# FNet mixing with windowed attention: the two lo-part differences of one weight tile are issued on DVE instead of GpSimd

## The chip, the core and the metric

The kernel runs on one core of a Trainium2 chip. Its time is the device time of one execution in microseconds (us). Before the change three runs gave 845.13, 845.97 and 846.19 us, a median of 845.97 us. The engines are called as the profile calls them: PE multiplies matrices, DVE (VectorE) and ACT (ScalarE) do elementwise work, POOL is GpSimd, and SP issues nearly all DMAs.

## The reference

```python
x = A_x                                              # 1 x 2048 x 512
g = sigmoid((x * gate_w).sum(-1, keepdims=True))
a = dft_seq_re @ (x @ dft_hid_re.T) - dft_seq_im @ (x @ dft_hid_im.T)
q, k, v = split(x @ wqkv)                            # 32 heads of 16
s = q @ k.T / 4, kept where 0 <= i - j < 256
b = softmax(s) @ v, heads joined, @ wo
return g * a + (1 - g) * b                           # 1 x 2048 x 512
```

## The kernel before, in words

Products of fp32 accuracy are made from fp32r pieces. Each operand X is split into `hi`, its value rounded to fp32r by a cast, and `lo = X - hi`, a difference. A product is then three matmuls (`TERMS`, L250): hi by hi, hi by lo and lo by hi. A weight tile (`raw`, 128x1024 fp32, two buffers) becomes a pair `hi`, `lo` (three buffers each) in four instructions: for each half of 512 columns one cast and one difference.

PE works through two streams at once. The dense stream (`dense`, L598) makes, in this order, the projections q and k of the first head group (`qk_proj(0, ss)`), the projection v of all rows (`v_proj`, sixteen calls of twelve matmuls of 512 columns each, into one PSUM tile `dv`), q and k of the second group (`qk_proj(1, ss, w)`, two chains of twelve matmuls, tiles `dqk`), the hidden transforms (`ab_proj`) and the sequence transforms. The attention stream makes for each query block n four score products (`s_pair`, L369), later their transposed form (`t_pair`) and the product with v (`pv`). The main loop interleaves them: `fill` takes dense matmuls between the attention's. Up to the block LAG = 19 the rhythm is one score matmul, then three dense ones. PE's order is written out by hand (`manual_schedule`, L993); DVE, ACT, POOL and SP are ordered by the framework's scheduler, and `behind(...)` (L68) ties an instruction to a place behind a named one of the same or another engine.

The PSUM tiles `d` of the dense stream have two buffers: a projection can begin when the one two before it has been evicted. A chain of q and k is evicted by ACT (`hi`, L88) and DVE (`lo`, L90 for k, L92 for q), a `dv` by ACT (L317). For each block DVE also makes the four masked scores (L371, from PSUM) and the padded weights of the next block's score matmuls (`make_pad`, L352, two instructions that read the SBUF tile `ring` and write the tile `pad`).

Small work is hung into the dense stream by a list `jobs`: `job` (L120) takes one entry off it at the third and ninth matmul of every twelve. `split_soon` (L111) puts the four instructions of one weight tile on the list: cast and difference of the first half, cast and difference of the second. On POOL's side it uses GpSimd up to block LAG (`masks` is still empty there) and DVE from then on. Each is issued through `late` (L588), which places it behind the last marked instruction of ACT and DVE, where its engine is one of these. For the second group's weights, at ss = 3, L623 sets an empty entry behind each of the four, so that they come twelve matmuls apart: in the `v_proj` of the row blocks 12, 13, 14 and 15. The second group's `qk_proj`, the first reader of the pair, follows at once.

The `raw` tile of these weights shares its two buffers with the tiles of `wi` (the imaginary hidden transform), which come in two loads, L631 and L641. The first is in place early. The second, called the second `wi` load here, takes the buffer of the second group's weights and so waits until their split has read it. Both `wi` tiles are split on POOL too. Their pieces are first read by `ab_proj(1, 0)`, whose matmuls begin at 108.6 us.

Of the kernel before, what the change touches and what calls it, by code (L numbers as in the profile page):

```python
# [32 lines left out]
def fnet_window_mix(ctx: ExitStack, tc: tile.TileContext, xT, x, wqk, wv, wr, wi, cr, ci, wo, gw, out):  # L33
    nc = tc.nc
# [23 lines left out]
    def f(ap):  # L58
        return ap.bitcast(F32)
# [7 lines left out]
    @contextmanager  # L67
    def behind(*engines):  # L68
        with ExitStack() as es:
            for e in engines:  # L70
                if e in last:
                    es.enter_context(tc.issue_after(last[e]))
            yield


    masks = []
# [19 lines left out]
    def load_raw(src):  # L96
        raw = st.tile([P, 1024], F32, name="raw", bufs=2)
        ld(raw, src)
        return raw
# [8 lines left out]
    jobs = []  # L108
    ended = []

    def split_soon(raw):  # L111
        hi = st.tile([P, 1024], F32R, name="hi")
        lo = st.tile([P, 1024], F32R, name="lo")
        for c in HALVES:
            jobs.append(lambda c=c: late(nc.scalar.copy if FIN else (nc.vector if masks else nc.gpsimd).tensor_copy,
                                         hi[:, c], raw[:, c]))
            jobs.append(lambda c=c: late((nc.vector if masks else nc.gpsimd).tensor_sub, lo[:, c], raw[:, c], f(hi[:, c])))
        return hi, lo

    def job(n):  # L120
# [26 lines left out]
    with tc.manual_schedule(engines={mybir.EngineType.Activation, mybir.EngineType.DVE, mybir.EngineType.SP}):  # L147
# [11 lines left out]
        for dk in range(DK):  # L159
            c = slice(dk * 256, dk * 256 + 256)  # L160
# [115 lines left out]
    def qk_proj(g, ss, w):  # L276
        for i in range(2):
            ps = ps_d.tile([P, 512], F32, name="dqk", tag="d")
            n = 0
            for dk in range(DK):  # L280
                c = dk * 256 + i * 128
                for a, b in TERMS:
                    nc.tensor.matmul(ps, w[a][:, c:c + 128], XT[dk, ss][:, b],  # L283
                                     start=n == 0, stop=n == 11)
                    n += 1
                    job(n)
                    if n < 12:
                        yield
            qk_evict(g, ss, i, ps)
            yield  # L290
# [22 lines left out]
    def v_proj(sb, w):  # L313
        ps = ps_d.tile([P, 512], F32, name="dv", tag="d")
        yield from row_proj(sb, w, ps)
        t = ev.tile([P, 512], F32, name="ev")
        mark("act", nc.scalar.copy(t, ps))  # L317
        ld(v_scr[sb // 2][sb % 2].rearrange("r a g x -> r (a g x)"), t)
        yield
# [182 lines left out]
    class Pieces:  # L502
# [8 lines left out]
        def split(self):  # L511
            if self.raw:
                k, raw = self.raw.pop(0)
                self.w[k] = split_soon(raw)
# [73 lines left out]
    def late(fn, *args):  # L588
        with behind("act", "dve"):
            return fn(*args)  # L590
# [7 lines left out]
    def dense():  # L598
# [10 lines left out]
        def x_job(ss, dk):  # L609
            late(split_x, ss, (dk,), ss == 1 or (None if ss == 3 else False))  # L610
            if dk % 2 and ss == 2:
                load_x(3, dk // 2)

        for ss in range(4):
            if ss < 3:
                for dk in range(DK):
                    jobs.append(lambda ss=ss, dk=dk: x_job(ss + 1, dk))
                    jobs.append(lambda: None)
            if ss:
                yield from qk_proj(0, ss, wq0)  # L620
            if ss == 3:
                w = split_soon(raw)
                jobs[:] = [j for split in jobs for j in (split, lambda: None)]  # L623
            for c in range(4):
                yield from v_proj(ss * 4 + c, wvs)
                have.add(("v", ss * 4 + c))
                if c == 1:
                    have.add(("qk", 0, ss))
                if ss == 2 and c == 2:
                    raw = load_raw(wqk[1])  # L630
                    wraw = [load_raw(wi[0])]  # L631
# [3 lines left out]
        for g in range(1, NG):  # L635
            for ss in range(4):
                yield from qk_proj(g, ss, w)
                have.add(("qk", g, ss))
                if g == 1:
                    if ss == 0:  # L640
                        wraw.append(load_raw(wi[1]))  # L641
                        ws = [split_soon(wraw[0])]
                    elif ss == 1:
                        ws.append(split_soon(wraw[1]))
                        raw = load_raw(wqk[2])
                elif g == 2:
                    if ss == 0:
                        raw = load_raw(wqk[3])
                        gate_soon(7)
                    elif ss == 1:  # L650
                        nextw = split_soon(raw)
                        wraw = [load_raw(wr[0])]
                    elif ss == 2:
                        wraw.append(load_raw(wr[1]))
                elif ss == 0:
                    ws = [split_soon(wraw[0])]
                elif ss == 1:
                    ws.append(split_soon(wraw[1]))
                    gate_load(4)
                elif ss == 2:  # L660
                    gate_load(5)
                else:
                    gate_soon(8)
# [9 lines left out]
            if g < 3:  # L673
                w = nextw
# [287 lines left out]


    stream = dense()
    quota = 0.0

# [150 lines left out]
```

## Time and profile before

| | |
|---|---|
| median of three runs | 845.97 us |
| the profiled execution's own time | 845.52 us |
| its span, first to last instruction | 843.6 us |
| granted clock of PE over the span | 1.000 |
| busy: DVE | 644.9 us (76%) |
| busy: ACT | 610.2 us (72%) |
| busy: POOL | 299.2 us (35%) |

Times in the rows count from the span's start. In a row of the timeline stand start, duration, engine, line and operation, the tile written and those read, the shape, and how many instructions were merged; in brackets the idle time of the engine ahead of it and what ended it. A matmul's duration contains its pipeline, so successive matmuls overlap, and the distance from start to start is what tells the rate.

### The profile page before, as it was taken

What the parts mean: (1) busy time and instruction counts of PE and PEld (TensorE: products, weight loads), DVE (VectorE), ACT (ScalarE), POOL (GpSimd) and SP (SyncE); (2) the same over time, 40 slices, a digit from 0 to 9 for tenths busy, and PEclk for the clock granted to TensorE, in tenths of its full rate; (3) what the DMA queues carried; (4) which work ended last, traced back from release to release, by engine and by line L of the source; (5) the groups of instructions that cost most, each with busy time, mean ns of one, the idle gap of its engine ahead of it and who ended that gap; (6) DMA issues with size and microseconds to landing.
All of it is one profiled execution on the core that took longest, in us unless ns stands there. A gap on an engine that the chain in (4) does not pass through costs nothing.

```text
span 843.6 us, 17198 instructions
## 1 busy us (share of the span) xinstructions
PE 838.4 (99%) x5322; PEld 697.5 (83%) x5322; DVE 644.9 (76%) x2082; ACT 610.2 (72%) x1832; POOL 299.2 (35%) x606
## 2 busy tenths in 40 slices
PE   9999999999999999999999999999999999999998
PEld 8887888888888888888888887878888878878997
DVE  5588978677879787787877876878987867666874
ACT  6487888878888897787977976867777865553430
POOL 8102332233232333242333243343232357756410
PEclk9999999999999999999999999999999999999999
DMA  8776678485765273544444557879874356456632
GB/s 310 238 225 179 219 247 278 165 246 215 221 221 184 58 225 108 178 124 121 140 150 136 166 149 229 288 223 300 284 216 140 99 179 203 140 184 205 217 132 94
DMA packets 94491, 161.03 MB, mean 191 GB/s; under 512 B 26816, under 2 KB 35520, under 8 KB 94400
## 3 DMA queue, kind: packets, MB, share of 16 engines
q1 hardware_dynamic: 93968, 159.28, 59.9%
q8 instruction: 42, 0.69, 0.3%
q10 hardware_dynamic: 432, 0.66, 0.2%
q14 instruction: 49, 0.40, 0.2%
HBM read 108.27 MB, written 51.64 MB: 190 GB/s over the span
## 4 chain that ended last, share of the span: by engine, by line
PE 98%; DVE 1%; DMA 0%; issue 0%; ACT 0%; DVEq 0%; ACTq 0%
PE dc L531 42%; PE dab L306 11%; PE dqk L283 10%; PE t L451 9%; PE s L369 8%; PE o L477 8%; PE dv L306 5%; PE t L926 5%; PE s L271 1%; DMA pt<-xT 0%; DVE pad L352 0%; PE s L389 0%; PE t L561 0%; ACT sm L374 0%; DVE sm L371 0%
## 5 line engine op out<-in xcount | busy, mean ns | idle before, releaser
L531 PE MATMUL dc<-big,hi 128*128 128x512 f32 x1020 | 344.6, 393 | 0.0
L371 DVE CUSTOM_DVE_ANT_0 sm<-s,mask 128x320 f32<-128x320 f32 (+4 forms) x512 | 235.2, 464 | 111.3 <-PE s L369 66.9
L374 ACT ACTIVATE sm<-sm,ml 128x320 f32<-128x320 f32 (+4 forms) x512 | 277.3, 543 | 58.3 <-DVE ml L371 53.7
L452 ACT ACTIVATE pt<-t 128x320 f32<-128x320 f32 (+4 forms) x392 | 159.5, 411 | 83.5 <-PE t L451 78.2
L531 PE MATMUL dc<-big,lo 128*128 128x512 f32 x510 | 200.2, 393 | 0.0
L531 PEld LDWEIGHTS dc<-big,hi 128*128 128x128 f32 x1020 | 179.3, 188 | 21.4
L456 POOL TENSOR_SCALAR_AFFINE_SELECT pt<-pt 128x128 f32<-128x128 f32 x196 | 77.0, 393 | 275.4 <-ACT pt L452 274.1
L451 PE MATMUL t<-ring,pad 128*128 128x320 f32 (+4 forms) x512 | 156.6, 306 | 0.0
L369 PE MATMUL s<-ring,pad 128*128 128x320 f32 (+4 forms) x512 | 155.0, 303 | 0.1
L352 DVE TENSOR_SCALAR pad<-ring,half 96x256 fp32r<-96x256 f32 x384 | 121.7, 363 | 5.2 <-PE t L451 4.9
L451 PEld LDWEIGHTS t<-ring,pad 128*128 128x128 f32 x512 | 96.1, 188 | 30.5 <-issue 9.1
L369 PEld LDWEIGHTS s<-ring,pad 128*128 128x128 f32 x512 | 96.2, 188 | 20.9 <-DVE ml L371 1.1
L531 PEld LDWEIGHTS dc<-big,lo 128*128 128x128 f32 x510 | 95.9, 188 | 11.9
L374 ACT ACTIVATION_READ_ACCUMULATOR sm<-sm,ml 128x1 f32 x512 | 97.4, 190 | 0.0
L590 DVE TENSOR_TENSOR lo<-raw,hi 128x512 fp32r<-128x512 f32 x137 | 95.1, 701 | 2.8 <-ACT hi L590 2.7
L306 PE MATMUL dab<-hi,big 128*128 128x512 f32 x256 | 88.9, 394 | 0.0
L283 PE MATMUL dqk<-big,hi 128*128 128x512 f32 x240 | 85.1, 393 | 0.0
L434 POOL TENSOR_SCALAR vpad<-vr,half 128x256 f32<-128x256 f32 x64 | 62.3, 986 | 62.3 <-PE o L477 29.6
L350 ACT ACTIVATE pad<-ring,half 96x256 fp32r<-96x256 f32 x128 | 66.7, 521 | 0.0
L456 POOL TENSOR_SCALAR_AFFINE_SELECT home<-home 128x128 f32<-128x128 f32 x60 | 34.5, 575 | 89.5 <-ACT home L452 87.0
L590 DVE CAST hi<-raw 128x512 fp32r<-128x512 f32 x126 | 53.7, 432 | 11.6 <-PE dc L531 10.6
L460 POOL TENSOR_SCALAR_AFFINE_SELECT pt<-pt 128x128 f32<-128x128 f32 x172 | 62.5, 363 | 0.0
(121 smaller groups left out, 1035.4 us busy)
## 6 DMA issues: line engine op xcount, KB each, us to landing
qk_scr<-home SPq DMA_DIRECT2D x32, 512.0 KB
ring<-qk_scr SPq DMA_DIRECT2D x32, 512.0 KB
raw<-cr SPq DMA_DIRECT2D x32, 512.0 KB
raw<-ci SPq DMA_DIRECT2D x32, 512.0 KB
r_scr<-ev SPq DMA_DIRECT2D x42, 256.0 KB
ab_scr<-home SPq DMA_DIRECT2D x20, 512.0 KB
big<-ab_scr SPq DMA_DIRECT2D x20, 512.0 KB
ring<-qk_scr SPq DMA_DIRECT2D x32, 256.0 KB
```

Source lines behind the costliest of these rows:

```text
L283: nc.tensor.matmul(ps, w[a][:, c:c + 128], XT[dk, ss][:, b], start=n == 0, stop=n == 11)
L306: nc.tensor.matmul(ps, XT[dk, ss][:, a, c * 128:(c + 1) * 128], wh[b], start=n == 0, stop=n == 11)
L352: mark(f"pad{i}", nc.vector.tensor_scalar(dst, src, half[:96, h:h + 1], None, op0=OP.mult))
L369: nc.tensor.matmul(ps[:, :w], PAD[0, n][:, p], ring[1][:, p, k0:k0 + w], start=True, stop=True)
L371: mark("dve", nc.vector.tensor_tensor_reduce(out=sm[:, :w], in0=ps[:, :w], in1=mask[:, WIN - w:], scale=1.0, scalar=3e38, op0=OP.add, op1= ...
L374: mark("act", nc.scalar.activation(sm[:, :w], sm[:, :w], AF.Exp, bias=nm[:, c], scale=-1.0, accum_out=l[:, c]))
L451: nc.tensor.matmul(ps[:, :w], PAD[1, n][:, p], ring[0][:, p, q0:q0 + w], start=True, stop=True)
L452: nc.scalar.activation(pt[:, p, :w], ps[:, :w], AF.Exp, scale=-1.0)
L456: nc.gpsimd.affine_select(a, a, pattern=[[0, 2], [2, 64]], compare_op=OP.is_ge, fill=0.0, base=1, channel_multiplier=-1)
L477: nc.tensor.matmul(OT[g, sb][32 * p:32 * p + 32, q - sb * 512:e - sb * 512], v2[:, p], pt[:, p, q - q0:e - q0], start=first, stop=kb == 8 ...
L531: nc.tensor.matmul(ps, w[a][:, i % 8 * 128:i % 8 * 128 + 128], ab[SC[i]][:, b], start=i == ends[0] and a + b == 0, stop=i == ends[1] and a ...
L590: return fn(*args)
```

## The change

`split_soon` gets a second argument. Where it is set, the two differences go to DVE whatever `masks` holds; the casts stay where they were. It is set in one of its calls, that for the second group's weights.

```diff
-    def split_soon(raw):
+    def split_soon(raw, on_dve=False):
         hi = st.tile([P, 1024], F32R, name="hi")
         lo = st.tile([P, 1024], F32R, name="lo")
         for c in HALVES:
             jobs.append(lambda c=c: late(nc.scalar.copy if FIN else (nc.vector if masks else nc.gpsimd).tensor_copy,
                                          hi[:, c], raw[:, c]))
-            jobs.append(lambda c=c: late((nc.vector if masks else nc.gpsimd).tensor_sub, lo[:, c], raw[:, c], f(hi[:, c])))
+            jobs.append(lambda c=c: late((nc.vector if on_dve or masks else nc.gpsimd).tensor_sub, lo[:, c], raw[:, c], f(hi[:, c])))
         return hi, lo
...
             if ss == 3:
-                w = split_soon(raw)
+                w = split_soon(raw, True)
                 jobs[:] = [j for split in jobs for j in (split, lambda: None)]
```

The orders of PE and ACT are the same in both kernels. On POOL, around the split of the second group's weights (`lo<-raw,hi` and `hi<-raw` are the instructions of all weight tiles; the first two casts are the second group's, the next ones those of `wi`), the difference between the two orders is:

```order
 L202 MEMSET ring_264 32x4x512
 L82 CAST big<-raw 128x512 x4
-L590 CAST hi<-raw 128x512 x2
-L590 TENSOR_TENSOR lo<-raw,hi 128x512 x2
-L590 CAST hi<-raw 128x512 x2
+L590 CAST hi<-raw 128x512 x4
 L590 TENSOR_TENSOR lo<-raw,hi 128x512
 L590 CAST hi<-raw 128x512
```

The two differences behind the first two casts are gone; the four casts stand in a row, and the three differences of `wi` keep their places.

On DVE the first of the two differences comes into the row block 13 of v. Before, from the last of the small transposed rows (L400; `ISA` is the masked score of L371 and the reading of its minimum) over the next pads (L352):

```order
L400 TENSOR_TENSOR mhl<-s,mhl 32x128
L371 ISA sm,ml<-s,mask 128x320
L371 ISA ml 128x1
L352 TENSOR_SCALAR pad_0_260<-ring_264,half 96x4x64 x2
L371 ISA sm,ml<-s,mask 128x320
L371 ISA ml 128x1
```

The same place now:

```order
L400 TENSOR_TENSOR mhl<-s,mhl 32x128
L371 ISA sm,ml<-s,mask 128x320
L371 ISA ml 128x1
L352 TENSOR_SCALAR pad_0_260<-ring_264,half 96x4x64 x2
L590 TENSOR_TENSOR lo<-raw,hi 128x512
L371 ISA sm,ml<-s,mask 128x320
```

The difference stands right behind a pair of pads. The second one stands in the same way behind the pair of pads two blocks later. On SP one load moves (`v_scr_119` and `v_scr_120` are stores of v, `raw<-wi` is the second `wi` load):

```order
 L56 DMA v_scr_119<-ev 128x512
 L56 DMA ring_264<-m_scr_141 4x4x512
+L56 DMA v_scr_120<-ev 128x512
 L56 DMA raw<-wi 128x1024
-L56 DMA v_scr_120<-ev 128x512 x2
+L56 DMA v_scr_120<-ev 128x512
 L56 DMA qk_scr_1_0_85<-home 128x2x512
 L56 DMA vr<-v_scr_113 128x4x64
```

The second `wi` load now stands behind the store of v's row block 14 instead of ahead of it, and waits for DVE instead of POOL.

## The prediction

> **What bounds the kernel now.** First the page's list of busy times, then the waits of PE alone.
>
> ```profile
> PE 838.4 (99%) x5322; PEld 697.5 (83%) x5322; DVE 644.9 (76%) x2082; ACT 610.2 (72%) x1832; POOL 299.2 (35%) x606
> ...
> PE dv L306 <- DVE home L90: 0.8, 1, 0.8
> ```
>
> PE is busy for 99% of the span, so an edit on DVE and POOL counts only where PE stands still for them. There is one such place in the list of PE's waits: a matmul of v waits once for DVE's eviction of a k chain (L90). The timeline of PE there, of which I took the score matmuls (one per round) and the matmul that waited:
>
> ```profile
> 68.01 0.31 PE L369 MATMUL s<-ring,pad 128*128 128x320 f32 x1
> 68.85 0.31 PE L369 MATMUL s<-ring,pad 128*128 128x320 f32 x1
> ...
> 69.23 0.40 PE L306 MATMUL dv<-hi,big 128*128 128x512 f32 x1
> 70.47 0.50 PE L306 MATMUL dv<-hi,big 128*128 128x512 f32 x1 [0.84 <-DVE home L90]
> 70.87 0.42 PE L369 MATMUL s<-ring,pad 128*128 128x320 f32 x1
> ...
> 72.05 0.42 PE L369 MATMUL s<-ring,pad 128*128 128x320 f32 x1
> ...
> 73.00 0.31 PE L369 MATMUL s<-ring,pad 128*128 128x320 f32 x1
> ...
> 73.84 0.31 PE L369 MATMUL s<-ring,pad 128*128 128x320 f32 x1
> ```
>
> A round of one score matmul and three of v takes 0.84 us (68.01 to 68.85, 73.00 to 73.84). From 68.85 to 73.00 there are three rounds, 2.53 us at that rate, and they took 4.15. So the stop cost **1.62 us**, not the 0.84 that the wait list shows: the two rounds behind it are slow too. Why was L90 late? DVE and POOL at the same moment, and DVE's pads one and three blocks away from it:
>
> ```profile
> 63.65 0.61 DVE L352 TENSOR_SCALAR pad<-ring,half 96x256 fp32r<-96x256 f32 x2
> ...
> 67.03 2.78 DVE L352 TENSOR_SCALAR pad<-ring,half 96x256 fp32r<-96x256 f32 x2
> 69.73 0.68 DVE L90 TENSOR_TENSOR home<-dqk,home 128x512 fp32r<-128x512 f32 x1
> ...
> 75.56 0.61 DVE L352 TENSOR_SCALAR pad<-ring,half 96x256 fp32r<-96x256 f32 x2
> 65.92 1.18 POOL L590 CAST hi<-raw 128x512 fp32r<-128x512 f32 x2 [28.20 <-PE dqk L283]
> 67.06 2.60 POOL L590 TENSOR_TENSOR lo<-raw,hi 128x512 fp32r<-128x512 f32 x2
> ```
>
> A pair of pads takes 0.61 us, this one 2.78, and it ends at 69.81, just behind POOL's two differences (67.06 to 69.66). They are the two that the change takes off POOL. The pads lost 2.17 us to them, L90 stood behind the pads, and PE's next `dv` needed the PSUM buffer that L90 frees: L90 ends at 70.41, PE goes on at 70.47. The Trainium skill, "SBUF — State Buffer", section "SBUF: two separate sides", calls this an exclusive lock: a GpSimd instruction and certain DVE ones share a port pair, and who comes second fully blocks. The 2.78 us agree.
>
> **The change part by part.** *POOL loses two differences*, 2.60 us. In their absence the pads run from 67.03 to about 67.64 (0.61), L90 to about 68.25. PE wants the buffer after its matmul of 69.23, at about 69.46, so there is 1.2 us to spare. The casts ahead (65.92 to 67.10) stay, and touch the pads' first 0.07 us only. Saved on PE's path: 1.62 us.
>
> *DVE gains two differences.* Their price on DVE, and DVE's load in the stretches that take them (columns: length, then busy time and count of PE, PEld, DVE, ACT, POOL, then clock and DMA):
>
> ```profile
> L590 DVE TENSOR_TENSOR lo<-raw,hi 128x512 fp32r<-128x512 f32 x137 | 95.1, 701 | 2.8 <-ACT hi L590 2.7
> 75.00:80.00 5.00, 5.00 (x25) 4.28 (x25) 3.87 (x17) 4.74 (x17) 0.34 (x1) 1.00 0.93 208
> 80.00:85.00 5.00, 5.00 (x26) 4.27 (x25) 3.43 (x14) 4.60 (x14) 2.09 (x3) 1.00 1.04 324
> 81.68 0.39 PE L283 MATMUL dqk<-big,lo 128*128 128x512 f32 x1
> 83.34 0.39 PE L283 MATMUL dqk<-big,lo 128*128 128x512 f32 x1
> ```
>
> That is 2 x 0.70 = 1.40 us. The first lands where DVE no longer makes up for 2.17 us of lost pads; the second, behind the pads that start at 78.87 in the old timeline, in a stretch with 1.13 + 1.57 = 2.70 us of idle DVE. Queued behind each are scores, for which PE has four PSUM buffers, more than two rounds of cover for 0.70 us. The casts that they wait for are done 4 us earlier. PE first reads a `lo` of these weights at 81.68, of the second half at 83.34 (old timeline), 3.2 us behind the end of the second difference. Cost on the path: 0; up to 1.40 us if that cover were gone.
>
> *The second `wi` load moves*, and this is what I can't put at nothing. It decides when POOL's remaining pair of differences runs. SP, POOL and DVE there:
>
> ```profile
> 72.75 1.41 SPq L56 DMA_DIRECT2D l_scr<-mhl  x2
> 74.20 3.83 SPq L56 DMA_DIRECT2D ring<-qk_scr  x4
> 78.14 0.53 SPq L56 DMA_DIRECT2D v_scr<-ev  x1
> 78.72 0.66 SPq L56 DMA_DIRECT2D ring<-m_scr  x1
> 79.47 0.38 SPq L56 DMA_DIRECT2D raw<-wi  x1
> 79.66 1.18 POOL L590 CAST hi<-raw 128x512 fp32r<-128x512 f32 x2 [9.99 <-PE dv L306]
> ...
> 85.81 0.75 POOL L590 CAST hi<-raw 128x512 fp32r<-128x512 f32 x1 [3.72 <-PE s L369]
> 86.53 2.55 POOL L590 TENSOR_TENSOR lo<-raw,hi 128x512 fp32r<-128x512 f32 x2
> 88.38 0.49 DVE L371 CUSTOM_DVE_ANT_0 sm<-s,mask 128x320 f32<-128x320 f32 x1 [0.33 <-PE s L369]
> ...
> 88.79 0.70 DVE L352 TENSOR_SCALAR pad<-ring,half 96x256 fp32r<-96x256 f32 x2
> 89.41 0.68 DVE L90 TENSOR_TENSOR home<-dqk,home 128x512 fp32r<-128x512 f32 x1
> ...
> 90.00:95.00 5.00, 5.00 (x27) 4.30 (x26) 4.95 (x21) 4.05 (x14) 2.24 (x3) 1.00 0.66 234
> 95.00:98.00 3.00, 3.00 (x16) 2.38 (x15) 2.92 (x10) 2.25 (x7) 1.43 (x2) 1.00 0.52 174
> 97.07 0.68 DVE L90 TENSOR_TENSOR home<-dqk,home 128x512 fp32r<-128x512 f32 x1
> 97.81 0.51 PE L283 MATMUL dqk<-big,hi 128*128 128x512 f32 x1
> ```
>
> The cast at 85.81 reads the second `wi` tile, whose load was issued at 79.47. The row names a score matmul as the releaser; since the cast reads nothing of it, I take the landing, 6.3 us after the issue, with the DMA engines fully busy from 80 to 85 (share 1.04). Behind the cast POOL's pair runs to 89.08, and its last 0.29 us meet the pads of 88.79, which end 0.09 us late. From those pads on DVE has no slack: 4.95 of 5.00 and 2.92 of 3.00 us busy until L90 ends at 97.75, and at 97.81 PE waits for exactly that. So whatever these pads lose, PE loses at 97.8.
>
> PE and DVE come 1.62 us earlier now; the question is by how much the landing does. For: SP's ring loads hang behind L400 (`l_scr`), which was late through the same stall, and come about 1.9 us earlier (L90 by 2.17, then a score that isn't ready yet). Against: one store of v, 256 KB, is now ahead of the load, 0.8 us at the 324 GB/s of that stretch. So the landing comes about 1.9 - 0.8 = 1.1 us earlier, POOL's pair comes 0.5 us later with respect to the pads, less 0.13 for the cast, which no longer meets pads (0.75 to 0.62). The pads lose about 0.4 us, which I take. Bounds: landing earlier by the full 1.62 or more, loss 0; landing not earlier at all, the pair ends at 89.08 + 1.49 = 90.57 and holds the second pad too: that ends at about 90.7 instead of 89.49, loss 1.2.
>
> **Sum:** 845.52 (the profiled run's own time, 843.6 span and 1.9 around it) - 1.62 + 0 + 0.4 = **844.3 us**. With the bounds, 843.9 to 845.1. The own time lies 0.45 us below the median of the three runs, which scatter by 1.1; I keep the own basis.
>
> **A rule against the change.** The same section of the Trainium skill's "SBUF — State Buffer" says that a DVE instruction with two SBUF inputs also takes the lock against a GpSimd one that reads SBUF. Both differences are such instructions, and the second, at 79.4 in the old timeline, meets POOL's casts of 79.66. If DVE is first, POOL waits 0.4 us, which is hidden; if POOL is first, the difference ends up to 1.2 us later and the `wi` load with it: by this rule the sum could become that of the second rival below.
>
> **The rivals.**
> *The block drifts onto both pads.* The landing is not earlier, both pads are held: 845.52 - 1.62 + 1.2 = 845.1. For it speaks the saturated DMA stretch; against it that the ring loads ahead of it do come earlier.
> *Slower than before.* The landing comes later than before in absolute time. For this the second difference must end late, so that the load, which now waits for DVE, is issued at about 80 instead of 78.5. That a DVE difference can be stretched by POOL shows in the view by tile:
>
> ```profile
> L590 DVE TENSOR_TENSOR lo<-raw,hi x137: 670/686/1228, 101.5 to 807.8; 128x512 fp32r<-128x512 f32 x137
> ```
>
> With 6.3 us to landing POOL's pair then falls on both pads whole; they lose up to 2.0 us (2.17 at 67.03), DVE has nothing to give, PE stops at L90's buffer as at 70.47 and pays the 0.6 of slow rounds again: 845.52 - 1.62 + 2.0 + 0.6 = 846.5, more if later pads are hit too. It decides once the landing is 0.8 us later than the old 85.8. Against it: the issue was at 79.47 before, and nearly the whole queue moves earlier.
> *The gain is whole.* The landing follows by 1.6 us or more: 843.9 or just below.
> *Nothing happens.* The pads of 67.03 are held by the casts and not by the differences, 845.5. The casts end at 67.10, so hardly.
>
> **How the numbers follow.** Forecast 0.58, whole gain 0.20, drift 0.09, slower 0.10, nothing 0.03. A change of 0.2% is about what can be told from none: 1.7 us, that is below 844.28 or above 847.66. The forecast lies at that bound, so half of it, 0.30, and the whole gain are faster: 0.50. Slower past the bound is most of the last rival but one that I give 0.10: 0.07, since later pads would have to be hit. The rest is within: 0.43. The range holds the forecast, the whole gain less half a microsecond for the scatter of runs, and the drift with as much above: 843.3 to 845.8.
>
> **What would show it.** Right: the pads near 67.03 take 0.6 to 0.7 us, PE has no wait at 69.5, the distance of the score matmuls there stays 0.84. Then the pads at about 87.2 (88.79 - 1.62) tell the rest: 1.0 us or so with POOL's pair on them, and a PE wait of some 0.4 us at about 96.2. Wrong: the stall at 69.5 is still there with POOL idle, or the second DVE difference holds scores until PE runs out of PSUM buffers, or the pads at 87.2 take over 2 us and PE stops behind L90 there.

## The result, and the profile after

| kernel | median of the runs (lowest to highest) | runs | ratio to before, 95% interval | span of the profiled execution |
|---|---|---|---|---|
| before | 845.80 us (844.87 to 847.39) | 22 | | 843.6 |
| after | 844.34 us (843.53 to 847.02) | 22 | 0.9986, 0.9979 to 0.9992 | 842.8 |

The kernel became faster by 1.2 us by the ratio (0.7 to 1.8 by the interval); the two medians differ by 1.46 us. The median of after lies 0.04 us from the predicted 844.3. The profiled execution of after took 844.79 us with 1.99 us of it around the span, that of before 845.52.

The waits of PE alone, of after (us in total, times, longest). The row that names L90 is gone:

```profile
PE s L271 <- ACT big L80: 1.0, 1, 1.0
PE dv L596 <- PEq L1109: 0.8, 1, 0.8
```

PE's timeline in after at the place of the old stop, of it the score matmuls, and the matmul that the prediction expected to wait at about 96.2, with the one ahead of it:

```profile
68.98 0.31 PE L369 MATMUL s<-ring,pad 128*128 128x320 f32 x1
69.82 0.31 PE L369 MATMUL s<-ring,pad 128*128 128x320 f32 x1
70.66 0.30 PE L369 MATMUL s<-ring,pad 128*128 128x320 f32 x1
...
96.83 0.39 PE L283 MATMUL dqk<-big,lo 128*128 128x512 f32 x1
97.22 0.50 PE L283 MATMUL dqk<-big,hi 128*128 128x512 f32 x1
97.56 0.31 PE L369 MATMUL s<-ring,pad 128*128 128x320 f32 x1
```

The rounds follow each other by 0.84 us through the place that had 4.15 us for three. DVE in the same execution: the pads at the old stop, L90 behind them, the two moved differences, then the pads and evictions further on:

```profile
68.00 0.61 DVE L352 TENSOR_SCALAR pad<-ring,half 96x256 fp32r<-96x256 f32 x2
68.53 0.68 DVE L90 TENSOR_TENSOR home<-dqk,home 128x512 fp32r<-128x512 f32 x1
...
72.49 0.68 DVE L590 TENSOR_TENSOR lo<-raw,hi 128x512 fp32r<-128x512 f32 x1
...
78.67 0.68 DVE L590 TENSOR_TENSOR lo<-raw,hi 128x512 fp32r<-128x512 f32 x1
...
84.76 0.96 DVE L352 TENSOR_SCALAR pad<-ring,half 96x256 fp32r<-96x256 f32 x2
88.06 0.61 DVE L352 TENSOR_SCALAR pad<-ring,half 96x256 fp32r<-96x256 f32 x2
...
95.57 1.00 DVE L352 TENSOR_SCALAR pad<-ring,half 96x256 fp32r<-96x256 f32 x3
96.49 0.68 DVE L90 TENSOR_TENSOR home<-dqk,home 128x512 fp32r<-128x512 f32 x1
```

And POOL's split instructions in after, and the later of its two pairs of `vpad` there (the padded v of L434), with what ended the idle time before them in brackets:

```profile
66.89 1.18 POOL L590 CAST hi<-raw 128x512 fp32r<-128x512 f32 x2 [28.62 <-PE dqk L283]
78.93 1.46 POOL L590 CAST hi<-raw 128x512 fp32r<-128x512 f32 x2 [10.86 <-PE dv L306]
80.36 1.30 POOL L590 TENSOR_TENSOR lo<-raw,hi 128x512 fp32r<-128x512 f32 x1
...
84.81 0.77 POOL L590 CAST hi<-raw 128x512 fp32r<-128x512 f32 x1 [3.15 <-DMA raw<-wi]
85.54 2.59 POOL L590 TENSOR_TENSOR lo<-raw,hi 128x512 fp32r<-128x512 f32 x2
...
94.28 1.89 POOL L434 TENSOR_SCALAR vpad<-vr,half 128x256 f32<-128x256 f32 x2 [2.31 <-DMA vr<-v_scr]
```

The pads at 68.00 take 0.61 us where they took 2.78, and L90 ends at 69.21. Two rows differ from what was expected. POOL's pair of differences (85.54 to 88.13) fell between two pairs of pads here: it met the pads of 84.76 (to 85.72) with its first 0.2 us and those of 88.06 with its last 0.07. The pads of 84.76 took 0.96 us, mostly beside the cast of 84.81, which took 0.77 instead of 0.61; DVE made up for it, since the next pads start 3.30 us behind them as in before (85.49 to 88.79). And PE's matmul of 97.22 came 0.16 us late (0.39 us behind its predecessor, not 0.23), instead of about 0.4. That lateness is not the loss that was forecast: the pads of 88.06 took 0.61 us, less than the 0.70 of before. L90 waited behind the three pads of 95.57, which took 1.00 us beside POOL's `vpad` (to 96.17); in before the same three read:

```profile
96.28 0.87 DVE L352 TENSOR_SCALAR pad<-ring,half 96x256 fp32r<-96x256 f32 x3
```

**Where the 0.8 us of span went.** Two executions are best laid against each other at fixed matmuls. The marks here are the first score matmul of the kernel, the 41st (66.16 us in before, 67.12 in after) and the 53rd, that is twelve rounds over the old stop, then the 20 rounds behind them and 18 more, which hold everything up to about 114 us. In us, from the starts of PE's L369:

| kernel | first score at | twelve rounds over the old stop | next 20 rounds | next 18 |
|---|---|---|---|---|
| before | 32.94 | 11.85 | 16.71 | 20.38 |
| after | 33.91 | 10.15 | 16.71 | 20.49 |

The stop is worth 1.70 us, 0.11 us is given back behind it. That this execution's span is only 0.8 us shorter is due to its start: its first score is 0.97 us later, behind a wait of 1.0 us for the first load's split (the row of L271 above), ahead of all that the change touches. The remaining 0.2 us lie in the rest of the kernel. In other executions of the very same kernel the first score comes at 33.06 and 33.10.

### The profile page after: what moved, and what is told of

Read it like the earlier page. It is cut to its first block, busy times and chain, and to the rows that moved or that the text cites. A ratio compares the mean times of both kernels' runs of the same rounds, so it can differ in the third digit from the quotient of the medians.

```text
span 842.8 us, 17198 instructions
## 1 busy us (share of the span) xinstructions
PE 837.9 (99%) x5322; PEld 697.7 (83%) x5322; DVE 642.7 (76%) x2084; ACT 609.6 (72%) x1832; POOL 294.7 (35%) x604
## 4 chain that ended last, share of the span: by engine, by line
PE 99%; DMA 1%; SPq 0%; ACT 0%; DVE 0%; issue 0%
PE dc L531 42%; PE dab L306 11%; PE dqk L283 10%; PE t L451 9%; PE s L369 9%; PE o L477 8%; PE dv L306 5%; PE t L926 5%; DMA pt<-wqk 1%; PE s L271 0%; PE s L389 0%; PE t L561 0%; SPq L56 0%; ACT big L80 0%; DVE rt L563 0%; ACT hi L162 0%
## 5 line engine op out<-in xcount | busy, mean ns | idle before, releaser
L371 DVE CUSTOM_DVE_ANT_0 sm<-s,mask 128x320 f32<-128x320 f32 (+4 forms) x512 | 235.0, 464 | 111.0 <-PE s L369 71.1
L369 PE MATMUL s<-ring,pad 128*128 128x320 f32 (+4 forms) x512 | 154.7, 302 | 0.0
L352 DVE TENSOR_SCALAR pad<-ring,half 96x256 fp32r<-96x256 f32 x384 | 118.8, 356 | 5.2 <-PE t L451 4.9
L369 PEld LDWEIGHTS s<-ring,pad 128*128 128x128 f32 x512 | 96.2, 188 | 19.9 <-ACT pt L452 0.4
L590 DVE TENSOR_TENSOR lo<-raw,hi 128x512 fp32r<-128x512 f32 x139 | 96.1, 699 | 2.5 <-ACT hi L590 2.4
L434 POOL TENSOR_SCALAR vpad<-vr,half 128x256 f32<-128x256 f32 x64 | 62.4, 986 | 62.0 <-PE o L477 29.5
L456 POOL TENSOR_SCALAR_AFFINE_SELECT home<-home 128x128 f32<-128x128 f32 x60 | 32.8, 548 | 90.7 <-ACT home L452 83.5
L590 DVE CAST hi<-raw 128x512 fp32r<-128x512 f32 x126 | 53.8, 433 | 12.4 <-PE dc L531 12.3
```

Of the source, the lines that this page charges most:

```text
L352: mark(f"pad{i}", nc.vector.tensor_scalar(dst, src, half[:96, h:h + 1], None, op0=OP.mult))
L369: nc.tensor.matmul(ps[:, :w], PAD[0, n][:, p], ring[1][:, p, k0:k0 + w], start=True, stop=True)
L371: mark("dve", nc.vector.tensor_tensor_reduce(out=sm[:, :w], in0=ps[:, :w], in1=mask[:, WIN - w:], scale=1.0, scalar=3e38, op0=OP.add, op1= ...
L456: nc.gpsimd.affine_select(a, a, pattern=[[0, 2], [2, 64]], compare_op=OP.is_ge, fill=0.0, base=1, channel_multiplier=-1)
```

## The experiments

The last columns of the table above are the measure in all of them, since spans move by a microsecond with the start. They come from one profiled execution of each kernel. Where an interval stands, the median is that of ten runs; for half_on_dve and pad_after_evict it does not tell the kernel from before, so what is said of these two rests on their profiles.

| kernel | median, us | ratio to before, 95% interval | first score | twelve rounds | next 20 | next 18 |
|---|---|---|---|---|---|---|
| third_on_pool | 845.73 | 1.0004, 0.9994 to 1.0013 | 33.41 | 11.85 | 16.71 | 20.37 |
| half_on_dve | 845.18 | 0.9991, 0.9982 to 1.0001 | 33.91 | 10.67 | 16.99 | 20.49 |
| pad_after_evict | 844.88 | 0.9990, 0.9981 to 1.0000 | 33.38 | 10.78 | 16.71 | 20.57 |
| wi2_thrice | 846.19 | 1.0005, 0.9995 to 1.0014 | 33.83 | 10.15 | 18.89 | 20.51 |
| half_turn_later | 846.86 (one run) | | 33.20 | 10.38 | 18.19 | 20.95 |
| casts_too | 844.99 (one run) | | 33.35 | 10.15 | 17.16 | 20.50 |
| no_spacing | 847.09 (one run) | | 33.93 | 10.15 | 17.62 | 20.72 |
| after_again | 844.28 (one run) | | 33.10 | 10.15 | 16.71 | 20.37 |
| no_spacing_timed | 845.45 | 0.9990, 0.9981 to 1.0000 | 33.51 | 10.15 | 17.70 | 20.86 |
| no_spacing_listed | 844.62 | 0.9982, 0.9973 to 0.9991 | 33.37 | 10.14 | 16.71 | 20.44 |
| pool_listed | 844.50 | 0.9979, 0.9970 to 0.9989 | 33.54 | 10.15 | 16.71 | 20.41 |
| after_timed | 844.49 | 0.9979, 0.9970 to 0.9988 | 33.06 | 10.15 | 17.09 | 20.50 |

Beside the first four, on the same chip, the median of before was 845.83 us, beside the last four 846.14; beside the single runs it ran once, in 846.66 us.

### Is it POOL's differences that hold the pads?

**third_on_pool**: before, with the second difference made twice, so that POOL has three in a row.

```diff
-    def split_soon(raw):
+    def split_soon(raw, again=False):
...
-            jobs.append(lambda c=c: late((nc.vector if masks else nc.gpsimd).tensor_sub, lo[:, c], raw[:, c], f(hi[:, c])))
+            def diff(c=c):
+                for _ in range(2 if again and c == HALVES[1] else 1):
+                    late((nc.vector if masks else nc.gpsimd).tensor_sub, lo[:, c], raw[:, c], f(hi[:, c]))
+            jobs.append(diff)
...
-                w = split_soon(raw)
+                w = split_soon(raw, True)
```

> The kernel before with GpSimd's second difference made twice (same values, 1.3 us more GpSimd work in the same place). Theory (only pads are held by GpSimd, one instruction each): both pads are already through when the third difference begins, and L90 and the scores, which read PSUM, are not held: PE stops at the same place for the same 1.6 us, time that of the kernel before within 0.3 us. Rival (GpSimd's differences slow DVE as a whole, PE loses 0.6 us per us of them): 0.8 to 1.3 us slower than the kernel before.

The timeline of POOL and DVE in third_on_pool (its lines stand three further down: L593 is L590, L355 is L352):

```profile
67.53 3.95 POOL L593 TENSOR_TENSOR lo<-raw,hi 128x512 fp32r<-128x512 f32 x3
67.50 2.78 DVE L355 TENSOR_SCALAR pad<-ring,half 96x256 fp32r<-96x256 f32 x2
70.21 0.67 DVE L90 TENSOR_TENSOR home<-dqk,home 128x512 fp32r<-128x512 f32 x1
```

The third difference runs on to 71.48 and costs nothing: the pads take 2.78 us as with two, and L90, which reads a PSUM buffer, takes 0.67 us beside it. So two pads are held by two differences, one by one, and L90 behind them is not held. The twelve rounds take 11.85 us as in before, and the ratio tells no difference. The stop is paid by the pads, not by the length of POOL's work.

**half_on_dve**: after, with only the first half's difference on DVE.

```diff
-            jobs.append(lambda c=c: late((nc.vector if on_dve or masks else nc.gpsimd).tensor_sub, lo[:, c], raw[:, c], f(hi[:, c])))
+            jobs.append(lambda c=c: late((nc.vector if on_dve and c == HALVES[0] or masks else nc.gpsimd).tensor_sub, lo[:, c], raw[:, c], f(hi[:, c])))
```

> The kernel after, but only the first half's difference is on DVE; the second stays on GpSimd right behind the casts. The order of SP is that of the kernel before. Theory (a GpSimd difference holds one pad instruction until it ends, L90 is late, and PE needs L90 only 1.2 us after its normal end): one difference holds the pads for about 1.3 us less than two, 0.9 us or so too long in all, L90 still ends before PE wants the buffer, so the whole gain is there: no PE wait near 70, three rounds of score matmuls there take 2.5 us, time 1.4 us below the kernel before. Rival 1 (PE loses in proportion to GpSimd's work): half the gain, 0.7 us. Rival 2 (the gain came from the moved load on SP): no gain.

POOL and DVE in half_on_dve:

```profile
68.15 1.36 POOL L590 TENSOR_TENSOR lo<-raw,hi 128x512 fp32r<-128x512 f32 x1
68.00 1.66 DVE L352 TENSOR_SCALAR pad<-ring,half 96x256 fp32r<-96x256 f32 x2
69.58 0.68 DVE L90 TENSOR_TENSOR home<-dqk,home 128x512 fp32r<-128x512 f32 x1
```

and the waits there, from 66 to 76 us:

```profile
PEld s L369 <- DVE ml L371: 0.7, 2, 0.5
PEld dv L306 <- DVE home L90: 0.2, 1, 0.2
```

One difference holds one pad: 1.66 us, between 0.61 and 2.78. L90 ends at 70.26 and its wait is down from the 0.84 us of before (1.3 on the weight loads) to 0.2 on the weight loads, so it did have the slack that the prediction gave it, nearly. But only 1.18 of the 1.70 us are won (11.85 - 10.67). The rest stands in the first row: two score matmuls wait for DVE to read an earlier score (L371), 0.7 us on the weight loads, as long as they do in before. These belong to the slow rounds that the prediction saw behind the stop and had no cause for: scores that wait for a PSUM buffer, because DVE, held at the pads, reads scores late. I had counted four buffers as cover.

**half_turn_later**: half_on_dve with the small transposition (L389), whose result takes one of those four buffers, moved from block 10 to block 11.

```diff
-    FIRST = (8, 1, ml_split), (10, 0, ml_turn), (10, 1, ml_rows), (12, 0, m_ring)
+    FIRST = (8, 1, ml_split), (11, 1, ml_turn), (11, 2, ml_rows), (12, 0, m_ring)
```

> The kernel with one difference on DVE and one on GpSimd, and in it the small transposed product of the row minima (L389, whose PSUM tile is one of the four that the scores use) made five scores later, so that no score buffer is taken while the held pads delay DVE. In the kernel without that move PE lost 0.5 us there though it never waited for L90: twelve score rounds took 10.67 us against 10.15 in the kernel after. Theory (the 0.5 us are scores that wait for a PSUM buffer, and three are left while L389's tile lives): the twelve rounds take 10.15 to 10.30 us. Rival (DVE's lateness of 1.05 us costs PE these 0.5 us anyway, or they are a slow restart of PE): 10.6 to 10.7 us.

The twelve rounds go from 10.67 to 10.38 us (10.15 to 10.30 were expected), which is 0.29 of the missing 0.52, and no score waits there any more. So the fourth buffer is part of the cause; the other 0.23 us stay open, since PE's weight loads still wait 0.3 us for L90 there, and this run cannot tell whether that is all of it. Its time is no measure of it: further on POOL's order fell differently (below) and cost 2 us.

**pad_after_evict**: before, with the held pads listed behind L90 in this one block.

```diff
-            if p == 0:
+            if p == (n == 10):
                 make_pad(0, n + 1)
+            if p == 0:
```

> The kernel before, both differences on GpSimd, but the one pair of pads in question is listed one score later, so that the eviction L90 stands ahead of it on DVE. Theory (PE stopped because L90 was queued behind the held pads): L90 ends near 67.8 of the old timeline, the pads are still held and end near 69.8; PE then waits for the pads of the next block's score matmul only, 0.2 us or so; 1.3 to 1.5 us of the 1.6 are won. Rival (GpSimd's differences themselves delay the eviction or PE): the stop stays at 1.6 us.

DVE in pad_after_evict:

```profile
67.51 0.69 DVE L90 TENSOR_TENSOR home<-dqk,home 128x512 fp32r<-128x512 f32 x1
68.52 1.73 DVE L352 TENSOR_SCALAR pad<-ring,half 96x256 fp32r<-96x256 f32 x2
```

and the waits from 66 to 76 us:

```profile
PEld s L369 <- DVE ml L371: 0.5, 1, 0.5
PEld s L369 <- DVE pad L352: 0.5, 1, 0.5
```

POOL's two differences run at 67.50 to 70.10 as ever, L90 is no longer behind a held instruction and takes 0.69 us beside them, and 1.07 of the 1.70 us are won without touching POOL. That is less than the 1.3 to 1.5 expected: the pads are still held until 70.25, and now PE waits for a pad and for a score. The new order has a second effect, though: the first difference now runs beside L90, which it does not hold, and the pads lose 1.12 us where they lost 2.17. So this run can't tell L90's place from the shorter hold; half_on_dve, with a hold of 1.05 us and L90 still behind it, wins 1.18 us. What it does show is that PE no longer waits for L90 and still loses 0.63 us through DVE's lateness with pads and scores. With both differences off POOL, both waits are gone.

**casts_too**: after, with the two casts on DVE as well.

```diff
-            jobs.append(lambda c=c: late(nc.scalar.copy if FIN else (nc.vector if masks else nc.gpsimd).tensor_copy,
+            jobs.append(lambda c=c: late(nc.scalar.copy if FIN else (nc.vector if on_dve or masks else nc.gpsimd).tensor_copy,
```

> The kernel after with the two casts of the same weights on DVE as well (0.42 us each), the first of them right behind the pads in question and ahead of L90. Theory (L90 may end 1.2 us late before PE waits, and nothing but pads is held by GpSimd): L90 ends 0.4 us later, PE does not wait, twelve score rounds take 10.15 us as in the kernel after, within 0.1; so it did not matter for PE that GpSimd keeps the casts. Rival (DVE is so full there that 0.4 us more ahead of L90 reaches PE): 10.4 us or more.

DVE in casts_too:

```profile
67.97 0.41 DVE L590 CAST hi<-raw 128x512 fp32r<-128x512 f32 x1
68.30 0.68 DVE L90 TENSOR_TENSOR home<-dqk,home 128x512 fp32r<-128x512 f32 x1
```

The first cast (0.41 us) stands between the pads and L90, so L90 runs from 68.30 to 68.98 instead of right behind the pads of 67.44, and PE does not notice: 10.15 us. The two casts and two differences, 2.2 us of DVE work by 0.41 + 0.42 + 2 x 0.68, cost nothing at this place. What it loses, it loses later.

### What do held pads cost further on?

**after_again** is after without an edit, for a second execution.

> The kernel after once more, unchanged, for how much one execution differs from the next. Theory: the twelve rounds take 10.15 us again (PE's stop is gone in every execution), while the start (first score matmul at 33.9 us in the first profile, 32.9 in that of the kernel before) and the second wi landing with respect to the pads (0.05 us behind the start of a pair, 0.3 in the kernel before) move by some tenths to 1 us. Rival (the 1.6 us were a matter of chance in the one profile): 11 us or more.

POOL and DVE in after_again:

```profile
85.24 2.56 POOL L590 TENSOR_TENSOR lo<-raw,hi 128x512 fp32r<-128x512 f32 x2
87.25 0.96 DVE L352 TENSOR_SCALAR pad<-ring,half 96x256 fp32r<-96x256 f32 x2
...
90.16 0.18 DVE L382 CAST mlh<-ml 128x64 fp32r<-128x64 f32 x1
...
95.56 0.68 DVE L90 TENSOR_TENSOR home<-dqk,home 128x512 fp32r<-128x512 f32 x1
```

Here is what was forecast, nearly to the digit: the pads at 87.25 (87.2), 0.96 us long (1.0), with POOL's pair on them until 87.80. But PE loses nothing (16.71 and 20.37, as in before). The reason is an instruction that I had not looked at, a small cast three scores further on. In before it reads:

```profile
91.45 0.40 DVE L382 CAST mlh<-ml 128x64 fp32r<-128x64 f32 x1
```

It took 0.22 us longer there, which hid in DVE's busy 4.95 of 5.00 us. So of the 0.26 us that the pads lose more than in before, 0.22 come back at L382, and L90 starts 8.31 us behind the pads' start instead of 8.28.

**wi2_thrice**: after, with the first difference of the second `wi` tile made three times, so that POOL's block reaches both of those pads.

```diff
-    def split_soon(raw, on_dve=False):
+    def split_soon(raw, on_dve=False, times=1):
...
+            def diff(c=c):
+                for _ in range(times if c == HALVES[0] else 1):
+                    late((nc.vector if on_dve or masks else nc.gpsimd).tensor_sub, lo[:, c], raw[:, c], f(hi[:, c]))
+            jobs.append(diff)
...
-                        ws.append(split_soon(wraw[1]))
+                        ws.append(split_soon(wraw[1], times=3))
```

> The kernel after, with the first difference of the second wi tile made three times on GpSimd (same values; two more of 1.3 us), so that GpSimd still runs when the pads near 88.1 come. Theory (from these pads on DVE has next to no slack until PE waits for L90 near 97.2): the second pad is held 0.9 to 1.0 us, L90 behind it ends that much later, and PE's stop near 97.2 grows from 0.3 to 1.0 or 1.3 us; time 0.8 to 1.0 us above the kernel after. Rival (DVE catches up as it did behind the pads of 84.76): PE's stop stays at 0.3 us, time that of the kernel after.

POOL and DVE in wi2_thrice (L593, L355 and L385 are L590, L352 and L382):

```profile
86.30 3.92 POOL L593 TENSOR_TENSOR lo<-raw,hi 128x512 fp32r<-128x512 f32 x3
92.04 1.29 POOL L593 TENSOR_TENSOR lo<-raw,hi 128x512 fp32r<-128x512 f32 x1
87.98 2.38 DVE L355 TENSOR_SCALAR pad<-ring,half 96x256 fp32r<-96x256 f32 x2
...
92.33 1.05 DVE L385 CAST mlh<-ml 128x64 fp32r<-128x64 f32 x1
```

and PE's waits that after does not have:

```profile
PE dqk L286 <- DVE home L90: 0.7, 1, 0.7
PE s L392 <- DVE mlh L386: 0.5, 1, 0.5
```

This is the slower rival, made to happen. The pads take 2.38 us, PE stops at L90's buffer as at the old stop, and POOL's last difference (92.04) then holds the small cast until 93.38, which lets PE's transposition wait. 2.18 us go in the next 20 rounds. The median is 1.85 us above after's (taken in another series, where before had 845.80 us beside 845.83 here), and the ratio tells no difference from before: with two differences more on the wrong instructions all of the gain is gone. Expected were 0.8 to 1.0 us; the pads alone lose 1.68 us over before, and the small cast 0.65.

These executions, with those of half_on_dve, casts_too, after_timed and after itself, can be laid side by side. In us; "L90 later" is the start of the second L90 behind the pads (97.07 in before) less the start of the pads, over the 8.28 of before, and "PE lost" is the sum of the last two columns of the table above over before's 37.09:

| kernel | pads | L382 | L90 later | PE lost |
|---|---|---|---|---|
| before | 0.70 | 0.40 | 0 | 0 |
| after | 0.61 | 0.18 | 0.15 | 0.11 |
| after_again | 0.96 | 0.18 | 0.03 | -0.01 |
| half_on_dve | 1.34 | 0.18 | 0.42 | 0.39 |
| after_timed | 1.45 | 0.18 | 0.51 | 0.50 |
| casts_too | 1.52 | 0.18 | 0.59 | 0.57 |
| wi2_thrice | 2.38 | 1.05 | 2.34 | 2.31 |

What L90 is late PE loses, within 0.04 us, in every row. In the five rows with held pads DVE has indeed no slack: what the pads and L382 together lose over before is what L90 is late, within 0.02 us. In after it is otherwise: its pads and L382 take 0.31 us less than in before and L90 gains nothing by it, but is 0.15 us late, and 0.13 of that are the three pads of 95.57 beside `vpad`. So lost time is passed on there, while saved time is not.

### Does the spacing matter?

**no_spacing**: after without the empty entries that spread the split's jobs over twice as many matmuls.

```diff
                 w = split_soon(raw, True)
-                jobs[:] = [j for split in jobs for j in (split, lambda: None)]
```

> The kernel after without the empty entries, so that each difference is listed six matmuls behind its cast and all four instructions lie within two row blocks of v. The first difference then stands behind L399, among the scores that make up for L90. Theory (the casts are done long before, the 0.7 us are hidden if the scores have buffers): PE loses 0 to 0.2 us more than in the kernel after, twelve rounds take 10.15 to 10.35 us. Rival (the distance of twelve matmuls is what hides the differences; DVE would wait for GpSimd's casts at the head of its queue): 10.5 us or more, with DVE idle ahead of a difference.

> The kernel without the empty entries, timed. Its one look had a stop that the kernel after lacks: GpSimd's three remaining differences stood in a row behind the landing of the second wi tile (3.88 us), held the pads of 84.78 for 2.20 us, L92 was late and PE stopped for 0.65 us at 87.6 and 0.37 at 98.4. Theory (this is the order of GpSimd, not chance): the same row of three and the same stops, 0.9 to 1.3 us above the kernel after, close to the kernel before. Rival (chance of one execution): the time of the kernel after.

POOL and DVE in no_spacing:

```profile
83.64 0.61 POOL L590 CAST hi<-raw 128x512 fp32r<-128x512 f32 x1 [3.52 <-DMA raw<-wi]
84.22 3.88 POOL L590 TENSOR_TENSOR lo<-raw,hi 128x512 fp32r<-128x512 f32 x3
84.78 2.20 DVE L352 TENSOR_SCALAR pad<-ring,half 96x256 fp32r<-96x256 f32 x2
```

and the two matmuls of PE that wait:

```profile
87.63 0.51 PE L283 MATMUL dqk<-big,hi 128*128 128x512 f32 x1 [0.48 <-DVE home L92]
98.38 0.50 PE L283 MATMUL dqk<-big,hi 128*128 128x512 f32 x1 [0.21 <-DVE home L90]
```

At the old stop nothing changes (10.15). But POOL now has the cast of the second `wi` tile ahead of the first `wi` difference. That cast waits for its load, all three remaining differences wait behind it, and then they come in a row on the pads of 84.78, which take 2.20 us; PE stops for evictions at 87.6 and 98.4. Timed, the kernel is at 845.45 us, 0.96 above after_timed. The empty entries were in the kernel before, and by the medians more than half of the gain is lost without them.

**no_spacing_listed** and **pool_listed** tie POOL's casts and differences to the order in which they are written (cast, difference, cast, difference), the first without and the second with the empty entries.

```diff
+    def listed(elsewhere, fn, *args):
+        if elsewhere:
+            return late(fn, *args)
+        with behind("pool"):
+            mark("pool", late(fn, *args))
...
-            jobs.append(lambda c=c: late(nc.scalar.copy if FIN else (nc.vector if masks else nc.gpsimd).tensor_copy,
-                                         hi[:, c], raw[:, c]))
-            jobs.append(lambda c=c: late((nc.vector if on_dve or masks else nc.gpsimd).tensor_sub, lo[:, c], raw[:, c], f(hi[:, c])))
+            jobs.append(lambda c=c: listed(masks, nc.scalar.copy if FIN else (nc.vector if masks else nc.gpsimd).tensor_copy,
+                                           hi[:, c], raw[:, c]))
+            jobs.append(lambda c=c: listed(on_dve or masks, (nc.vector if on_dve or masks else nc.gpsimd).tensor_sub,
+                                           lo[:, c], raw[:, c], f(hi[:, c])))
```

> The same kernel without the empty entries, with GpSimd's casts and differences tied to the order in which they are listed, so that both differences of the first wi tile are made ahead of the landing and only a cast and one difference follow it. Theory (the spacing matters through GpSimd's order alone, not by where DVE's differences stand): the block behind the landing is 1.9 us instead of 4.5, it holds at most one pad pair for up to 1.3 us, PE's stops of 0.65 and 0.37 are gone or under 0.3 in all, time that of the kernel after within 0.3. Rival (the place of DVE's differences costs it): stops as in the kernel without the empty entries, 0.9 us or more above the kernel after.

> The kernel after with GpSimd's casts and differences tied to the order in which they are listed. The second difference of the first wi tile then runs near 81.5 to 82.8, where it holds the pads of 81.4 for 0.7 us and DVE has idle time; behind the landing only a cast and one difference are left. Theory (PE pays for held pads only behind 84.5, and then for what exceeds some 0.4 us): no PE stop left at 87 to 98 but the 0.1 of the kernels with the pads clear; 0 to 0.3 us below the kernel after, 1.5 to 1.7 below the kernel before. Rival (the pads held at 81.4 reach PE as those at 67 did): a stop of 0.3 us or more near 82 to 85, slower than the kernel after.

> The kernel after once more, timed beside the three others on the same chip. Theory: 1.2 to 1.6 us below the kernel before; twelve score rounds at the old stop in 10.15 us; how many tenths the pads near 84.8 or 88.1 lose to GpSimd differs from execution to execution, and PE pays for them only above some 0.4 us.

With the order tied, no_spacing's stops are gone (16.71 and 20.44) at the same spacing, so it was POOL's order that cost it, and the median is 0.83 us below no_spacing_timed. pool_listed holds the pads of 81.08 for 1.85 us and PE loses 0.03 us in all: at that place DVE does make up for it, other than at 87. It takes 844.50 us beside the 844.49 of after_timed, where 0 to 0.3 us less was expected; after_timed is 1.65 us below before. No version tried is faster than after.

## Why the prediction was right, step by step

**The stop.** Right, in cause and nearly in size: 1.70 us for the predicted 1.62. That POOL's differences hold the pads, one for one, is shown by third_on_pool, half_on_dve and after together (two or three, one and no difference: 2.78, 1.66 and 0.61 us). How the stop divides between L90 and the rest is less sure: by the rows of before PE stood for L90 from about 69.46 to 70.47, 1.0 of the 1.70 us, while pad_after_evict takes L90's wait away but halves the hold as well. What the prediction took over without a cause, the slow rounds, is at least in part the wait for score buffers seen in half_on_dve, of which half_turn_later removes 0.29 us. (The pads of 75.56 that the prediction compares with stand two blocks behind, not three; that changes nothing.)

**The casts.** Right that they are not what held these pads: they stay, end at 68.07 in after, and the pads of 68.00 take 0.61 us. The rival in which nothing happens falls with it. It is their place that makes them harmless: the cast of 84.81 in after does hold pads.

**DVE's two differences.** Right at a cost of zero: 0.68 us each, and the twelve rounds with both casts on DVE as well are no longer (10.15). The argument by four score buffers was too generous in general, since held pads ahead of L90 do make scores wait for them in half_on_dve; at the places where the differences stand it held.

**The rule weighed against the change.** The second difference (78.67 to 79.35) did meet POOL's casts of 78.93, and DVE was first. The pair of casts took 1.46 us, where it takes 1.17 or 1.18 us without a DVE difference beside it (half_on_dve, third_on_pool). That DVE's difference holds them agrees with the lock of two SBUF inputs in the Trainium skill, "SBUF — State Buffer", section "SBUF: two separate sides"; a wait for the whole 0.42 us that the two ran side by side, which a full block would be, was not measured: the casts lost 0.28, where the prediction said 0.4. It was hidden, as the prediction had it for that case. The `wi` load was released by it at once, as SP's rows of after show:

```profile
77.98 0.33 SPq L56 DMA_DIRECT2D v_scr<-ev  x1
79.38 0.34 SPq L56 DMA_DIRECT2D raw<-wi  x1
```

**The give-back of 0.4 us.** This was the weak step, at the words "whatever these pads lose PE loses at 97.8". The forecast of the landing was good: in after_again POOL's pair ends at 87.80 (89.08 - 1.1 - 0.13 = 87.85 was forecast), and the pads take 0.96 us. But the loss was counted against a DVE without slack, and before had 0.22 us of it in the longer L382. The other error is one of kind. The cast that follows the landing came at 84.81, 84.67 and 85.12 us in three executions of after, and PE itself is 0.8 us earlier or later by its start, while the landing did not follow that (84.81 with the late start, 84.67 with an early one). So the give-back is a draw for each execution: 0.11, 0.0 and 0.50 us, 0.2 on the mean of the three, where the prediction had one number. Only the 0.50 comes from the pads that it named; the 0.11 of after comes from the three pads of 95.57 beside POOL's `vpad`, which the prediction did not count with. The sum with the measured terms, 845.52 - 1.70 + 0.2, is 844.0; the median is 844.3, and the own time that the sum started from lay 0.3 us below the median of the 22 runs of before. Two errors, 0.08 on the stop and 0.2 here, both towards a time too long, and that basis make up the agreement to 0.04 us, so it is partly luck.

**The rivals.** The whole gain is what after_again shows, after nearly so, and after_timed shows somewhat more than the forecast's loss; all lie in the range given, which by its own words would be 843.4 to 845.6. The slower rival did not happen, but its mechanism is real: with wi2_thrice and no_spacing POOL's remaining differences do land on both pads of a pair, and PE stops. It was kept away by the landing, which came 0.7 to 1.1 us earlier than in before although the load is behind one more store.

## What to carry to other kernels

When an engine that is far from full stops the one that is full, look on it for an instruction that takes several times its usual time, and for what runs beside it on the other engines; moving 2.6 us off an engine that was busy for a third of the span won what those 2.6 us had held up, not what they took. Ask of an instruction that holds another which ones it lands on: the same difference costs nothing on the pads of 81, half a microsecond on those of 87, and 1.7 us at 67 for two of them. A column that says 4.95 of 5.00 busy is not proof of no slack, since held time counts as busy: compare the single instructions with their usual durations first.

## What was not expected of the hardware

- A GpSimd difference of 1.30 us holds one DVE pad until it ends, and the next difference the next pad: three in a row held two pads and let the 0.67 us eviction from PSUM run beside the third (third_on_pool).
- It also works the other way: DVE's difference of 0.68 us held POOL's pair of casts by 0.28 us (1.46 for 1.18), in each of three executions of after.
- The small cast L382 takes 0.40 us in before and 0.38 or 0.39 in two other kernels, while POOL's `vpad` runs (1.84 to 1.93 us for two); in after_again it takes 0.18 with the same `vpad` beside it. The three pads near 95.6 are held by `vpad` in after (1.00 us) and not in after_again (0.87). What decides between the two stays open.
- The first score comes between 32.94 and 33.93 us in these profiles, ahead of everything that the change touches; a single execution can't tell changes below a microsecond by its span.
